# Keys by token for four units: made with TensorE transposes and a ScalarE copy instead of loaded

## The chip, the cores and the metric

One core of a Trainium2 chip runs the whole program; the other cores are idle. The metric is the device time of one execution in microseconds. Five engines work from queues of their own: TensorE (PE: weight loads and matmuls), VectorE (DVE), ScalarE (ACT), GpSimd (POOL) and SyncE (SP), which here issues all loads and stores. Engines wait for each other and for loads through semaphores.

## The reference, cut to what matters

Three stages follow one another; the change lies in the first.

```python
# 1. retention: batch 4, heads 8, sequence 576, head size 64
scores = (1 / sqrt(64)) * q @ k.transpose(0, 1, 3, 2)
gamma = 1 - 2.0 ** (-5 - arange(8))                  # one per head
Dmat = where(i >= j, gamma ** (i - j), 0)            # causal decay
x = (scores * Dmat) @ v                              # -> 2304 tokens x 512
# 2. h = x @ w_in (512 x 2048); g = h * sigmoid(1.702 * h); x = g @ w_out
# 3. h = x @ w_in2 (512 x 1024); solu = h * softmax(h); layer norm * g_ln; out = . @ w_out2
```

The outputs are 2304 x 512 numbers in fp32.

## The kernel before, in words

The retention is done in chunks. The 32 heads of the batch go two at a time: a *unit* is two heads (2 x 64 features on the 128 partitions), there are 16 units, and two units make a *pair* (`k` in `run`, 0 to 7). The sequence of 576 is four chunks of 128 tokens and a rest of 64. For a unit TensorE computes the following blocks:

- `scores` (line 394, tile `s`): inside each chunk, keys times queries, 4 chunks x 2 heads. VectorE masks them into SBUF (line 399).
- `states` (line 358, tile `T`): for each chunk, the sum over its tokens of key times value. This needs k *by token* (tokens on the partitions), while scores need k *by feature*. It also needs v scaled by the decay, which ScalarE does in place (`scale_v`, lines 343 and 347).
- `within` (line 409, tile `o`): masked scores times v.
- `across` (lines 424, 430 and 436, tiles `o` and `e`): the running state, which VectorE makes from `T` with a scan (line 367, once for a pair), times the queries. GpSimd has multiplied the queries by their decay before (`decay_q`, lines 328 and 333).
- `last_scores` (line 375, tile `e`): the scores of the rest of 64 tokens.

ScalarE or VectorE then copies the results from PSUM into `xb` (`take`, lines 447 to 454).

Each unit comes from memory in two loads that SyncE issues in order (`load_unit`, line 210). Part 0 is q and k by feature, 1152 columns. Part 1 is k by token (512 columns from `CKN`), and v (576 columns from `CV`): 1088 columns. So k is loaded twice, in two layouts. Six units have buffers (`NU`); unit 6 takes the buffers of unit 0 when these are free, and so on.

Nothing reorders the program: each engine's queue is filled in the order in which `run` calls the functions. Pair 0 has an order of its own (`EARLY = 1`): scores, T and `within` of unit 0 with short runs of idle matmuls between them (`spin`, tile `warm`), then scores and T of unit 1, the end scores, scores of unit 2, `within` of unit 1, `across` of the pair, then the T blocks of units 2 and 3, and scores of unit 3. Before the loop ScalarE scales the v of units 0 and 1; that of units 2 and 3 follows in pair 0. PSUM has four banks for `warm`, `T`, `o`, `e` (`bank`) and four for scores and others (`ybank`); a new tile in a bank waits until the one before is read.

The first part of stage 2 follows on directly: from the third pair on the first weights are loaded and converted beside the retention.

Of the kernel before, what the change touches and what calls it, by code (L numbers as in the profile page):

```python
# [13 lines left out]
ALU = mybir.AluOpType  # L14
# [3 lines left out]
B, H, S, D = 4, 8, 576, 64  # L18
# [5 lines left out]
P = 128  # L24
CH = 128
NCH = 4
# [15 lines left out]
CQ, CK = 0, S  # L42
CKN, CV = 2 * S, 2 * S + NCH * P
NV = 2 * NCH + 1
CATT = CV + NV * D
# [57 lines left out]
_M = {}  # L103
# [10 lines left out]

NU = 6
PLAIN = (0, 2)
EARLY = 1
NPAIR = B * NP // 2
IN_AT = [_M["att"], _M["att"] + CATT] + [_M["y"] + i * CATT for i in range(4)]
# [33 lines left out]
class Build:  # L153
# [56 lines left out]
    def load_unit(self, u, part):  # L210

        t = IN_AT[u % NU]
        a, b = ((0, CKN), (CKN, CATT))[part]
        self.load(t + a, self.att_in[u, :, a:b])

    def load_raw(self, dst, src):
# [118 lines left out]
    def scale_v(self, *units):  # L335
# [8 lines left out]
        for u in units:  # L344
            v = self.un(u)[0][:, CV:CATT]
            d = self.const("vdec")[:, u % NP * 3:u % NP * 3 + 3]
            self.nc.scalar.mul(v[:, n:], v[:, n:], d[:, 2:3])

    def states(self, u, pt):


        t = self.un(u)[0]
        n = NCH * D
        out = pt[:, u % 2 * n:(u % 2 + 1) * n].rearrange("r (e c) -> r c e", c=NCH)
        for c in range(NCH):
            for a, h in enumerate(self.rows(u)):
                w = slice(c * P + a * D, c * P + (a + 1) * D)
                self.nc.tensor.matmul(  # L358
                    out[h, c], t[:, CKN + w.start:CKN + w.stop], t[:, CV + w.start:CV + w.stop],
                    start=True, stop=True, skip_group_check=True,  # L360
                )

# [78 lines left out]
    def take(self, u, o, part):  # L441
# [3 lines left out]
        x = self.x(u)[:, n:S] if part else self.x(u)[:, 0:n]  # L445
        if u not in PLAIN:
            nc.scalar.copy(x, o[:, 0:LAST] if part else o)
# [249 lines left out]
    def run(self):  # L697
        nc = self.nc
# [7 lines left out]
        def spin(n):  # L706
            for _ in range(n):
                nc.tensor.matmul(wb[:, 0:P], warm, warm, start=True, stop=True)
# [9 lines left out]
        def load_w():  # L718
            f, h = raws.pop(0)
            n = slice(h * SLICE, (h + 1) * SLICE)  # L720
            self.load_raw(self.wraw[f][:, n], self.w1_in[f][:, h * DM:(h + 1) * DM])
# [2 lines left out]
        self.load_consts()  # L724
        self.load_unit(0, 1)
        self.load_decays(1, 1)
        self.fill_scan()
        for u in range(1, NU):
            for part in range(2):
# [6 lines left out]
        for f, h in halves:  # L736
            t = T_START[f % 2]
# [3 lines left out]
        for f in range(3, FH):  # L741
            t = T_START[f % 2]
# [4 lines left out]
            self.bg += [(0, p, "split") for p in self.split_weight(f, t)]  # L747


        self.scale_v(0)  # L750
        self.scale_v(1)
        self.decay_q(1)
        self.decay_q(3)
        for k in range(NPAIR):
            u = 2 * k
            nxt = k + 1 < NPAIR
            early = k < EARLY
            if k + 2 < NPAIR:
                self.decay_q(u + 4, u + 5)
            if nxt and not early:  # L760
                self.scale_v(u + 2, u + 3)
            if k != 1:
                self.scores(u)
            if k == 0:
                spin(4)
                pt = self.bank("T0")
                self.states(u, pt)
                spin(4)
                o = [self.bank("o0")]
                self.within(u, o[0], True)  # L770
                self.scores(u + 1)
                self.states(u + 1, pt)
                ends = self.bank("e0")
            else:
                self.scores(u + 1)
                if early:
                    pt = self.bank(f"T{k}")
                    for i in range(2):
                        self.states(u + i, pt)
                o = [self.bank(f"o{u}")]  # L780
                ends = self.bank(f"e{k}")
            if early:
                self.last_scores(k, ends)
                self.last_masks(k, ends)
                self.scan(k, pt)
                self.scores(u + 2)
            o.append(self.bank(f"o{u + 1}"))
            if early:
                for i in range(k == 0, 2):
                    self.within(u + i, o[i], True)  # L790
            if not nxt:
                self.split_x(0, 1, 0)
                self.split_x(0, 1, 1)
            self.background((0, 0, 0, 0, 2, 2, 2, 3)[k], True, nxt)
            ends = [ends, self.ybank(f"e{u + 1}")]
            self.across(k, o, ends, not early)
            if nxt and k >= EARLY - 1:
                self.last_scores(k + 1, ends[0])
                if early:
                    self.scale_v(u + 2, u + 3)  # L800
                pt = self.bank(f"T{k + 1}")
                self.states(u + 2, pt)
            for i in range(2):
                self.take(u + i, ends[i], True)
            if not nxt:
                self.emit_h(0, 0, 0, nc.vector, True)
                self.background(0)
            if not early:
                for i in range(2):
                    self.within(u + i, o[i], False)  # L810
            if nxt and k >= EARLY - 1:
                self.states(u + 3, pt)
                self.last_masks(k + 1, ends[0])
                self.background(k > 3)
                self.scan(k + 1, pt)
            for i in range(2):
                self.take(u + i, o[i], False)
                self.staged.add((4, u + i))
            if nxt and k < EARLY - 1:
                self.scale_v(u + 2, u + 3)  # L820
            for i in (u + NU, u + 1 + NU):
                if i < 2 * NPAIR:
                    for part in range(2):
                        self.load_unit(i, part)
            for _ in range((0, 0, 1, 1, 1, 1, 2, 2)[k]):
                load_w()
            if 2 < k < 7:
                self.split_x(0, 0, k - 3)
        prev, held = None, []
        for g, j, f in STEPS:  # L830
# [35 lines left out]
            if prev is not None:  # L866
                self.emit_y(*prev)
                pg, pj, pf = prev
                if pj == NB - 1:
# [3 lines left out]
                    elif pg == 2:  # L873
                        b = SLOT_OF[pf % FH]
# [179 lines left out]
```

## Time and profile before

| | us |
|---|---|
| median of 3 runs | 669.01 (668.78 to 669.54) |
| profiled execution | 669.22 |
| its span, first to last instruction | 667.4 |
| TensorE busy, share of the span | 658.9, 99% |
| VectorE busy | 487.1, 73% |
| GpSimd busy | 252.3, 38% |
| ScalarE busy | 232.7, 35% |

The profile is of one execution. Its page has busy times by engine, the span in 40 slices, the DMA queues, the chain of work that ended last, and groups of instructions. A busy TensorE is not TensorE at its peak, since matmuls overlap and their ends are modelled. One fp32 matmul of the program shows as two records (x16 is eight matmuls), a transpose as one. The retention ends at about 62 us of the span; the rest is stages 2 and 3.

### The profile page before, as it was taken

The numbers are of one execution on the slowest core, as the hardware profiler recorded it, in microseconds if no ns is written. First come the engines' busy times: TensorE is split into PE (matmuls) and PEld (weight loads), VectorE is DVE, ScalarE is ACT, GpSimd is POOL, SyncE is SP. The second block draws the span as 40 slices with busy tenths as digits, with TensorE's granted clock in tenths as the row PEclk, the third lists the DMA queues.
The fourth block names the chain that finished last, engine by engine and source line by source line (L and its number), as shares of the span: only waits on it lengthen the run. The fifth ranks groups of instructions, "written<-read, shape, count | busy, mean of one in ns | idle before, by whom it ended". The sixth has DMA issues, their size and how long they took to land.

```text
span 667.4 us, 10473 instructions
## 1 busy us (share of the span) xinstructions
PE 658.9 (99%) x4086; PEld 572.9 (86%) x4086; DVE 487.1 (73%) x769; ACT 232.7 (35%) x498; POOL 252.3 (38%) x268
## 2 busy tenths in 40 slices
PE   9999999999999999999999999999999999999998
PEld 8888888899888889998888888899878888888887
DVE  3678788688787866687675675467799987887780
ACT  2565544432112134121111211265545433543331
POOL 3465665534224149240220311289744322431200
PEclk9999999999999999999999999999999999999999
DMA  8998500012222210022211200000000000000001
GB/s 341 418 416 334 190 0 1 1 33 94 95 72 87 75 52 1 1 95 95 81 48 62 63 1 0 1 1 4 2 16 33 17 17 31 32 17 16 32 32 48
DMA packets 15025, 49.35 MB, mean 74 GB/s; under 512 B 1664, under 2 KB 2560, under 8 KB 14976
## 3 DMA queue, kind: packets, MB, share of 16 engines
q1 hardware_dynamic: 14976, 48.68, 20.0%
q8 instruction: 32, 0.52, 0.3%
q14 instruction: 17, 0.14, 0.1%
HBM read 43.96 MB, written 4.72 MB: 73 GB/s over the span
## 4 chain that ended last, share of the span: by engine, by line
PE 88%; DVE 5%; DMA 2%; issue 2%; ACT 1%; POOL 1%; SPq 0%; DVEq 0%; POOLq 0%; ACTq 0%
PE yp L523 28%; PE h L490 28%; PE o L688 14%; PE h L597 10%; DMA mem<-in_att 2%; PE zT L661 2%; PE s L394 2%; PE o L409 2%; PE T L358 1%; PE o L424 1%; DVE mem L603 1%; DVE mem L636 1%; DVE mem L562 1%; DVE mem L498 0%; ACT gs L500 0%
## 5 line engine op out<-in xcount | busy, mean ns | idle before, releaser
L490 PE MATMUL h<-xs,w 128*128 128x512 f32 (+1 forms) x960 | 212.1, 369 | 1.5 <-POOL xs L471 1.5
L523 PE MATMUL yp<-gs,w 128*128 128x512 f32 (+1 forms) x960 | 211.1, 368 | 0.3 <-ACT gs L500 0.3
L490 PEld LDWEIGHTS h<-xs,w 128*128 128x128 f32 x960 | 175.1, 188 | 26.6 <-POOL xs L471 4.0
L523 PEld LDWEIGHTS yp<-gs,w 128*128 128x128 f32 x960 | 175.0, 188 | 23.9 <-DVE mem L531 0.7
L471 POOL TENSOR_TENSOR xs<-xb,xs 128x384 fp32r<-128x384 f32 (+3 forms) x96 | 93.7, 1003 | 208.3 <-ACT xs L470 208.2
L497 ACT ACTIVATE mem<-h 128x512 f32<-128x512 f32 (+1 forms) x80 | 44.4, 555 | 257.3 <-PE h L490 257.2
L498 DVE TENSOR_TENSOR mem<-h,mem 128x512 f32<-128x512 f32 (+1 forms) x80 | 50.8, 636 | 86.2 <-ACT mem L497 86.0
L688 PE MATMUL o<-w,zs 128*128 128x512 f32 (+1 forms) x456 | 102.9, 382 | 0.0
L688 PEld LDWEIGHTS o<-w,zs 128*128 128x128 f32 x456 | 81.3, 188 | 15.1
L503 DVE TENSOR_TENSOR gs<-mem,gs 128x512 fp32r<-128x512 f32 (+1 forms) x80 | 68.2, 852 | 13.0 <-ACT gs L500 6.4
L259 POOL TENSOR_TENSOR w<-mem,w 128x512 fp32r<-128x512 f32 x34 | 45.9, 1377 | 25.2 <-ACT w L254 25.2
L559 POOL TENSOR_TENSOR ys_s<-mem,ys_s 128x256 fp32r<-128x256 f32 x36 | 35.0, 984 | 51.9 <-ACT ys_s L558 41.8
L502 DVE CAST gs<-mem 128x512 fp32r<-128x512 f32 (+1 forms) x69 | 41.6, 603 | 6.6
L597 PE MATMUL h<-wt,ys_s 128*128 128x512 f32 x162 | 41.3, 390 | 0.0
L603 DVE TENSOR_TENSOR mem<-h,mem 128x512 f32<-128x512 f32 x36 | 24.6, 687 | 21.1 <-PE h L597 12.5
L597 PEld LDWEIGHTS h<-wt,ys_s 128*128 128x128 f32 x162 | 30.3, 188 | 6.2
L648 POOL TENSOR_TENSOR mem<-mem 128x1 f32<-128x1 f32 x18 | 10.3, 572 | 64.7 <-DVE mem L647 64.7
L470 ACT CAST xs<-xb 128x384 fp32r<-128x384 f32 (+3 forms) x96 | 34.6, 432 | 0.0
L399 DVE SCALAR_TENSOR_TENSOR mem<-s,mem 128x512 f32<-128x512 f32 x32 | 21.9, 740 | 9.9 <-PE s L394 9.9
L671 DVE TENSOR_TENSOR zs<-zT,zs 128x512 fp32r<-128x512 f32 x36 | 23.1, 684 | 7.7 <-ACT zs L670 7.7
L597 PE MATMUL h<-wb,ys_a 128*128 128x512 f32 x108 | 27.6, 391 | 0.2 <-ACT mem L606 0.2
L640 DVE TENSOR_TENSOR mem<-mem 128x1024 f32<-128x1024 f32 x18 | 24.7, 1374 | 3.7 <-ACT mem L638 3.7
(82 smaller groups left out, 726.1 us busy)
## 6 DMA issues: line engine op xcount, KB each, us to landing
mem<-in_att SPq DMA_DIRECT2D x16, 576.0 KB, 7.6
mem<-in_att SPq DMA_DIRECT2D x16, 544.0 KB, 8.2
wraw<-in_w SPq DMA_DIRECT2D x16, 512.0 KB, 9.2
mem<-in_w SPq DMA_DIRECT2D x16, 512.0 KB, 3.7
out<-mem SPq DMA_DIRECT2D x17, 256.0 KB, 2.0
mem<-in_w2in SPq DMA_DIRECT2D x8, 512.0 KB, 3.7
mem<-in_w2out SPq DMA_DIRECT2D x8, 512.0 KB, 3.7
out<-mem SPq DMA_DIRECT2D x2, 128.0 KB, 1.7
```

The costliest lines, as they stand in the source:

```text
L259: nc.gpsimd.tensor_tensor(lo[:, c], w[:, c], f32(hi[:, c]), ALU.subtract)
L470: nc.scalar.copy(t[:, 0, done:done + n], x)
L471: nc.gpsimd.tensor_tensor(t[:, 1, done:done + n], x, f32(t[:, 0, done:done + n]), ALU.subtract)
L490: nc.tensor.matmul(h[:, 0:width], a[:, w], x[:, b, 0:width], start=(n == 0), stop=(n == 3 * KB - 1))
L497: nc.scalar.activation(g, h[:, 0:width], AF.Sigmoid, scale=1.702)
L498: nc.vector.tensor_tensor(g, h[:, 0:width], g, ALU.mult)
L502: nc.vector.tensor_copy(gs[:, 0], g)
L503: lo_engine.tensor_tensor(gs[:, 1], g, f32(gs[:, 0]), ALU.subtract)
L523: nc.tensor.matmul(o, a[:, w], gs[:, b], start=(first and i == 0), stop=(last and i == 2))
L559: nc.gpsimd.tensor_tensor(ys[:, 1], src, f32(ys[:, 0]), ALU.subtract)
L597: nc.tensor.matmul(o, a[:, l, k], m[:, w], start=(start and i == 0), stop=(stop and i == 5), skip_group_check=True,)
L688: nc.tensor.matmul(o[:, 0:n], z[:, a, k], b[:, c:c + n], start=(k == 0 and i == 0), stop=(k == FB - 1 and i == 2),)
```

## The change: k by token from k by feature, for units 0 to 3

For units 0 to 3 (`TURNED`) part 1 of the load begins at `CV` and leaves k by token out. In its place `turn_k` transposes the four chunks of k by feature on TensorE, into one PSUM bank (tile `kn`), and ScalarE copies the bank, 128 x 512, to where the load used to put it. For a transpose an identity matrix is needed; GpSimd makes it from the constant `tri` (a triangle of ones) by subtracting the triangle shifted by one column. In units with an odd number the two heads stand the other way round on the partitions, so `states` picks its columns by `h` there. The scalings of v move behind these copies in ScalarE's queue. Units 4 to 15 are loaded as before.

```diff
+TURNED = 4
@@ load_unit
-        a, b = ((0, CKN), (CKN, CATT))[part]
+        a, b = ((0, CKN), (CKN if u >= TURNED else CV, CATT))[part]
@@
+    def turn_k(self, u):
+        nc = self.nc
+        t = self.un(u)[0]
+        ident = self.at(_M["g"] + 2 * P, P)
+        pt = self.bank(f"kn{u}")
+        for c in range(NCH):
+            w = slice(c * P, (c + 1) * P)
+            nc.tensor.transpose(pt[:, w], t[:, CK + c * CH:CK + (c + 1) * CH], ident)
+        nc.scalar.copy(t[:, CKN:CV], pt)
@@ states
+                k = CKN + (c * P + h.start if u < TURNED else w.start)
-                    out[h, c], t[:, CKN + w.start:CKN + w.stop], t[:, CV + w.start:CV + w.stop],
+                    out[h, c], t[:, k:k + D], t[:, CV + w.start:CV + w.stop],
@@ run
+        ident, tri = self.at(_M["g"] + 2 * P, P), self.const("tri")
+        nc.gpsimd.tensor_copy(ident[:, 0:1], tri[:, 0:1])
+        nc.gpsimd.tensor_tensor(ident[:, 1:], tri[:, 1:], tri[:, 0:P - 1], ALU.subtract)
         self.fill_scan()
...
-        self.scale_v(0)
-        self.scale_v(1)
         self.decay_q(1)
...
+            if k == 0:
+                self.turn_k(0)
+                self.scale_v(0)
             if k != 1:
                 self.scores(u)
...
                 self.within(u, o[0], True)
+                self.turn_k(1)
+                self.scale_v(1)
                 self.scores(u + 1)
...
                 self.scan(k, pt)
+                self.turn_k(2)
                 self.scores(u + 2)
...
                 if early:
-                    self.scale_v(u + 2, u + 3)
+                    self.scale_v(u + 2)
+                    self.turn_k(3)
+                    self.scale_v(u + 3)
                 pt = self.bank(f"T{k + 1}")
                 self.states(u + 2, pt)
```

ScalarE's queue before, from the scalings of unit 0 to the first results of pair 0. Line 343 scales the four chunks of one head, line 347 the rest of 64 tokens; the names in brackets are the semaphores that a row waits for, and DMAHW ones are loads.

```order
L343 ACTIVATE mem<-mem 128x4x64 [waits DMAHW2_49,DMAHW1_49]
L343 ACTIVATE mem<-mem 128x4x64
L347 ACTIVATE mem<-mem 128x64
L343 ACTIVATE mem<-mem 128x4x64 [waits DMAHW5_49]
L343 ACTIVATE mem<-mem 128x4x64
L347 ACTIVATE mem<-mem 128x64
L343 ACTIVATE mem<-mem 128x4x64 [waits DMAHW0_49]
L343 ACTIVATE mem<-mem 128x4x64
L343 ACTIVATE mem<-mem 128x4x64 [waits DMAHW3_49]
L343 ACTIVATE mem<-mem 128x4x64
L347 ACTIVATE mem<-mem 128x64 x2
L447 COPY xb<-e_225 128x64 [waits PE_49]
```

The same place after the change, units 1 to 3. Line 359 is the copy of the transposed k, and the lines that were 343, 347 and 447 are 344, 348 and 460.

```order
L359 COPY mem<-kn_181 128x512 [waits PE_49]
L344 ACTIVATE mem<-mem 128x4x64 [waits DMAHW5_49]
L344 ACTIVATE mem<-mem 128x4x64
L348 ACTIVATE mem<-mem 128x64
L359 COPY mem<-kn_218 128x512 [waits PE_49]
L344 ACTIVATE mem<-mem 128x4x64 [waits DMAHW0_49]
L344 ACTIVATE mem<-mem 128x4x64
L348 ACTIVATE mem<-mem 128x64
L359 COPY mem<-kn_273 128x512 [waits PE_49]
L344 ACTIVATE mem<-mem 128x4x64 [waits DMAHW3_49]
L344 ACTIVATE mem<-mem 128x4x64
L348 ACTIVATE mem<-mem 128x64
```

Each unit's scalings, which waited for a load alone, now stand behind a copy that waits for TensorE.

TensorE's queue before, at the end of pair 0: the end scores of units 2 and 3 (line 375), the T blocks of units 2 and 3 (line 358), and the scores of unit 3 (line 394).

```order
L375 MATMUL e_196<-mem 64x64 [waits DMAHW2_49,Pool_49]
L375 MATMUL e_196<-mem 64x64
L358 MATMUL T_256<-mem 64x64 [waits DMAHW0_49,PE_49,Activation_49]
L358 MATMUL T_256<-mem 64x64 [waits Activation_49]
L358 MATMUL T_256<-mem 64x64 x6
L358 MATMUL T_256<-mem 64x64 [waits DMAHW3_49,Activation_49]
L358 MATMUL T_256<-mem 64x64 [waits Activation_49]
L358 MATMUL T_256<-mem 64x64 x6
L394 MATMUL s_0_294<-mem 128x128 [waits Pool_49]
```

The same place after: line 358 is now the transpose, line 371 the T blocks, line 388 the end scores, line 407 the scores.

```order
L388 MATMUL e_210<-mem 64x64 [waits DMAHW2_49,Pool_49]
L388 MATMUL e_210<-mem 64x64
L358 MATMUL kn_273<-mem 128x128 x4
L371 MATMUL T_282<-mem 64x64 [waits DVE_49,DMAHW0_49,PE_49,Activation_49]
L371 MATMUL T_282<-mem 64x64 [waits Activation_49]
L371 MATMUL T_282<-mem 64x64 x6
L371 MATMUL T_282<-mem 64x64 [waits DMAHW3_49,Activation_49]
L371 MATMUL T_282<-mem 64x64 [waits Activation_49]
L371 MATMUL T_282<-mem 64x64 x6
L407 MATMUL s_0_320<-mem 128x128 [waits Pool_49]
```

The four transposes of unit 3 stand directly ahead of the T blocks of units 2 and 3, and the T block of unit 3 waits for what ScalarE does behind them.

## Rows read from the trace of the kernel before

**Rows 1.** The page: busy us of each engine, share, instructions.

```profile
PE 658.9 (99%) x4086; PEld 572.9 (86%) x4086; DVE 487.1 (73%) x769; ACT 232.7 (35%) x498; POOL 252.3 (38%) x268
```

**Rows 2.** By stretch: busy us (instructions) of each engine, granted clock, DMA share, GB/s.

```profile
5.40:20.00 14.60, 13.66 (x234) 11.79 (x233) 7.34 (x14) 5.56 (x15) 3.69 (x8) 1.00 1.01 401
20.00:62.00 42.00, 40.42 (x898) 38.04 (x901) 32.68 (x55) 24.57 (x69) 24.85 (x32) 1.00 1.02 417
62.00:667.40 605.40, 600.48 (x2946) 518.77 (x2942) 446.94 (x701) 201.08 (x413) 222.07 (x223) 1.00 0.12 41
```

**Rows 3.** The chain of waits, 0 to 60 us: start, us, what.

```profile
8.47 9.80 DMA mem<-in_att
...
18.34 0.31 POOL mem L328
...
18.65 1.23 DVE mem L367
...
20.02 1.00 PE o L424 x24
...
24.53 1.99 PE s L394 x32
```

**Rows 4.** TensorE in order of time: start, us, engine, line, what [idle before].

```profile
5.45 1.16 PE L394 MATMUL s<-mem 64*128 64x128 f32 x16
6.54 1.16 PE L708 MATMUL warm<-mem 128*128 128x128 f32 x8
7.63 0.95 PE L358 MATMUL T<-mem 128*64 128x64 f32 x16
8.51 1.16 PE L708 MATMUL warm<-mem 128*128 128x128 f32 x8
11.71 0.68 PE L358 MATMUL T<-mem 128*64 128x64 f32 x16
12.33 0.45 PE L375 MATMUL e<-mem 64*64 64x64 f32 x8
16.27 0.69 PE L358 MATMUL T<-mem 128*64 128x64 f32 x16
17.47 1.08 PE L358 MATMUL T<-mem 128*64 128x64 f32 x16 [0.51 <-ACT mem L343]
18.48 1.16 PE L394 MATMUL s<-mem 64*128 64x128 f32 x16
```

**Rows 5.** ScalarE in order of time: scalings of unit 3, a copy from PSUM.

```profile
16.91 0.91 ACT L343 ACTIVATE mem<-mem 128x256 f32<-128x256 f32 x2 [3.27 <-DMA mem<-in_att]
18.29 0.58 ACT L447 COPY xb<-o 128x512 f32<-128x512 f32 x1
```

**Rows 6.** GpSimd and VectorE in order of time.

```profile
0.73 0.95 POOL L200 MEMSET mem<- 128x1024 f32 x1 [0.29 <-POOLq L1044]
4.89 1.21 POOL L204 COPY mem<-mem 128x192 f32<-128x192 f32 x4 [3.21 <-DMA mem<-in_consts]
8.59 0.30 POOL L328 TENSOR_TENSOR mem<-mem 128x64 f32<-128x64 f32 x1 [2.49 <-DMA mem<-in_att]
8.85 1.09 POOL L333 TENSOR_TENSOR mem<-mem 128x512 f32<-128x512 f32 x1
18.65 1.22 DVE L367 TENSOR_TENSOR_SCAN mem<-mem,T 128x512 f32<-128x512 f32 x1 [1.77 <-POOL mem L328]
```

**Rows 7.** The page: the instruction queue (packets, MB, share); DMA issues (KB, median us to landing).

```profile
q8 instruction: 32, 0.52, 0.3%
...
mem<-in_att SPq DMA_DIRECT2D x16, 576.0 KB, 7.6
mem<-in_att SPq DMA_DIRECT2D x16, 544.0 KB, 8.2
```

**Rows 8.** TensorE and ScalarE at 481 us: eight transposes, the next block, the copy.

```profile
481.16 1.03 PE L661 MATMUL zT<-mem 128*128 128x128 f32 x8
481.95 0.48 PE L597 MATMUL h<-wt,ys_a 128*128 128x512 f32 x1
...
481.79 0.59 ACT L670 CAST zs<-zT 128x512 fp32r<-128x512 f32 x1 [2.74 <-PE zT L661]
```

**Rows 9.** TensorE in order of time: `across` of pairs 2, 3 and 7.

```profile
26.45 1.00 PE L424 MATMUL o<-mem 64*64 64x128 f32 x24
32.77 1.00 PE L424 MATMUL o<-mem 64*64 64x128 f32 x24
60.98 1.00 PE L424 MATMUL o<-mem 64*64 64x128 f32 x24
```

**Rows 10.** The chain of waits, 30 to 60 us: what it calls issue.

```profile
34.68 0.36 issue
...
40.91 0.24 issue
...
53.23 0.39 issue
...
59.15 0.52 issue
```

**Rows 11.** Waits of TensorE from 62 us on: us in total, times, longest.

```profile
PE h L490 <- POOL xs L471: 1.5, 2, 0.8
PE yp L523 <- ACT gs L500: 0.3, 1, 0.3
PE h L597 <- ACT mem L606: 0.2, 1, 0.2
```

## The prediction

> **What bounds the kernel now.** I read the page's busy table first: TensorE is busy 658.9 of 667.4 us [rows 1], so nearly everything that is added to TensorE's own queue, or put in front of it, is paid in full, and a load matters only where TensorE waits for it. The table by stretch says where that could be: loads run at 401 GB/s from 5.4 to 20 us, at 417 GB/s until 62 us, and at 41 GB/s in the 605 us after that [rows 2]. The change touches the first 20 us alone. The chain of waits follows a load there up to 18.27 us, then a scan on VectorE, and TensorE from 20.02 us on [rows 3], which would make loads the bound of the start. The rows of TensorE in order of time say less. Its blocks follow one another from 5.45 us to the T block at 16.27, and it loses time at three places [rows 4]. The T block of unit 0 lasts from 7.63 to 8.51 us, 0.88, where an undisturbed one goes from 11.71 to 12.33, 0.62: 0.26 us lost. The T block of unit 3 would begin at 16.27 + 0.62 = 16.89 and end at 17.51; it ends at 18.48, 0.97 us late, because ScalarE's two scalings of v begin only at 16.91, when their load has landed [rows 5]. And `across` at 20.02 waits for the scan that ends at 18.65 + 1.22 = 19.87 [rows 6]; 18.48 + 1.09 (a block of scores, 5.45 to 6.54) would be 19.57, so 0.45 us. The chain names a GpSimd operation at 18.34 as what released this scan; the T block itself ends at 17.47 + 1.08 = 18.55, just ahead of 18.65, and is the likelier releaser.
>
> So loads cost TensorE about 1.7 us here, not the 10 us that the chain puts to them.
>
> **What is removed.** Part 1 of units 0 to 3 loses 512 of its 1088 columns: of 544 KB [rows 7], 288 KB stay. 256 KB are 0.262 MB, at 417 GB/s 0.63 us for each unit; the v of unit 3, and every load behind it while the queue stays full, lands 4 x 0.63 = 2.5 us sooner. Of this TensorE can take back at most those 1.7 us.
>
> **What is added on TensorE.** 16 transposes of 128x128. The kernel has such transposes late in the program: eight go from 481.16 to the start of the next block at 481.95, so 0.10 us each [rows 8]. Four take 0.4. A change of the block's shape costs too: one block of scores takes 1.09, a double one 1.99 [rows 3, 4], so one change is 2 x 1.09 - 1.99 = 0.2. Unit 0's four stand where the shape changes anyway; for units 1 to 3 I add 0.2 each. In all 4 x 0.4 + 3 x 0.2 = 2.2 us, all of it in TensorE's queue.
>
> The Trainium skill gives a transpose inside a kernel about 275 ns ("TensorE: Matmul & The Clock Gate", Part 4: PE-mode transpose). The row here agrees with that as the length of one, and shows that eight in a row overlap; taken one behind the other, 16 would be 4.4 us instead of 1.6 before changes of shape.
>
> **What is added in front.** *The identity.* GpSimd makes it once the constants have landed, 4.89 today [rows 6]: a copy of one column and a subtraction of 127. There is no such row; a multiplication takes 0.30 with 64 columns and 1.09 with 512 [rows 6], so about 0.4, and with a column's copy 0.5 (between 0.3 and 1.1 for both). Transposes then start near 5.6 instead of 5.45: 0.2 us, between 0 and 0.7. The table that GpSimd fills afterwards has its rows' 0.95 and 1.2 still ahead of 8.59, when it is next wanted.
>
> *The copy and the scalings.* ScalarE's order becomes copy, scale, scale for each unit (its rows are shown with the change). A 128x512 copy from PSUM takes 0.58, the two scalings 0.91 [rows 5]. T needs all three. Before, a unit's scalings ran as soon as its v had landed, under TensorE's other work; now they stand behind a copy that waits for TensorE. From the start of the last transpose to the end of the second scaling: 0.27 (one transpose) + 0.08 (hand-over: the copy at 481.79 behind a group that ends near 481.7 [rows 8]) + 0.58 + 0.91 = 1.84 us.
>
> **The sum, as lateness of TensorE against today.** Unit 0: 0.2 for the identity, 0.4 for transposes, and the 0.26 of T's wait gone: +0.35. Unit 1: transposes 0.6, so +0.95; the last one starts at about 11.4, the scalings end at 13.2, where T could begin at 11.71 + 0.95 = 12.66; +0.5, so +1.45. Unit 2: transposes 0.6; its copy hides under scores and `within`; +2.05. Unit 3: its transposes, 0.6 more, stand directly ahead of the T block of unit 2, which begins at 16.27 + 2.65 = 18.9. The last one starts at about 18.65, the scalings end at 18.65 + 1.84 = 20.5. T of unit 2 covers 0.6 of that, the rest is bare: T of unit 3 goes from 20.5 to 21.1, where it ends at 18.48 today: **+2.6 us**. The wait for the load is gone, and a longer one for ScalarE has come in its place. Scan and `across` follow, at 22.6 instead of 20.02. Bounds: with no cost for a change of shape and a free identity the same steps give +2.1; with the identity at 0.7, +3.1.
>
> **Behind 20 us.** Is this paid to the end? From 26.45 to 32.77 a pair of units takes 6.32 us with TensorE full; from 32.77 to 60.98 four pairs take 28.21, which is 2.93 more than 4 x 6.32 [rows 9]. That excess might give something back. The chain puts it to no engine: gaps called issue, 0.36, 0.24, 0.39 and 0.52 us, inside blocks [rows 10]. TensorE's list of waits after 62 us, where loads are few, has none [rows 11], and there is a queue that loads instructions, 32 packets, 0.52 MB [rows 7]. I take the gaps as TensorE waiting for its instructions behind a deep queue of data; that is an inference. This queue becomes shallower: loads are 2.5 us sooner, and TensorE frees the buffers for later units 2.6 us later, together 5.1 of the 7.6 us from issue to landing [rows 7]. So the excess shrinks by something between nothing and 2.9. No row shows a half-full queue, and the queue stays busy through most of the stretch; I take 1.1, a good third. +2.6 - 1.1 = +1.5. After 62 us nothing absorbs it: TensorE is full but for 2.0 us of waits [rows 11], which hang on the same work.
>
> The profiled execution took 669.22 us, 667.4 of it span and 1.8 around it, 0.2 above the median of 669.01. 669.0 + 1.5 = 670.5.
>
> **Rivals.**
> *The gaps close (no change).* If instructions arrive in time once the queue is shallow, all 2.9 come back: 669.0 + 2.6 - 2.9 = 668.7, or 669.7 with two thirds. For it: no such gap with an idle queue. Against: from 20 to 32 us TensorE ran the same blocks with loads at the same rate and lost nothing, so a busy queue alone isn't enough for a gap, nor then perhaps its absence.
> *Loads are the bound (faster).* If the chain is right and copies and scalings hide, TensorE gets back 1.7 us of waits against 2.2 + 0.2 of transposes and identity, +0.7, and with 2.5 of the 2.9 from the gaps it is -1.8: 667.2. It decides from the second pair's `across` at 20.9 or sooner. Against it: T of unit 3 has only one T block, 0.6 us, to hide 1.84 behind.
> *Transposes in series (slower by more).* If each of the 16 waits out the 0.27 us of the one before, they add 16 x 0.17 = 2.7, and the gaps give back 1.1: 669.0 + 2.6 + 2.7 - 1.1 = 673.2. It decides from 0.2 us between starts on. Against it: the eight at 481 us.
>
> **How the numbers follow.** The forecast, +0.7 to +2.6 (669.7 to 671.6), has 0.50; gaps that close 0.27; loads as the bound 0.11; series 0.07; gaps that grow, above 671.6, 0.05. A measurement of this kernel tells about 0.2%, 1.3 us, from no change, so 670.35 is the line. Of the forecast's half 0.37 lies above it; with the last two, slower has 0.49. Same takes 0.13 and 0.25 of the closing gaps, 0.38; faster 0.02 and 0.11, 0.13. The range, 668.7 to 672.2, leaves out loads as the bound and the series, 0.18, and little else.
>
> **What would show it.** Right: each four transposes within 0.45 us; ScalarE's copy of unit 3 and two scalings that end near 20.5, TensorE idle about 1 us ahead of the T block of unit 3 and named as waiting for ScalarE, `across` near 22.6; from there to the block that is at 60.98 today, some 1.1 us less than today's 40.96. Wrong: that `across` at or before 20.9, so that the copy is hidden; or the same 40.96 us behind it (nothing given back), or 38.0 (all).

## The result, and the profile after

| | before | after |
|---|---|---|
| median, runs side by side | 669.16 us (668.78 to 670.35) | 672.42 us (672.11 to 674.0) |
| ratio | | 1.0054 (95%: 1.0044 to 1.0064) |
| profiled execution, span | 669.22, 667.4 | 672.41, 670.6 |

The kernel became slower by 0.54%, 3.3 us on the medians and 3.2 us on the spans. The forecast was 670.5, its range 668.7 to 672.2: the direction came as foretold, the size lies above the range.

The page after, beside [rows 1]: busy us, share, instructions.

```profile
PE 660.4 (98%) x4102; PEld 573.7 (86%) x4102; DVE 486.9 (73%) x769; ACT 234.9 (35%) x502; POOL 252.7 (38%) x270
```

TensorE's busy time grew by 1.5 us and the span by 3.2, so half of the loss is time in which TensorE stands still. The table by stretch after, with the columns of [rows 2], says where.

```profile
5.40:20.00 14.60, 14.04 (x216) 11.77 (x216) 6.20 (x12) 5.85 (x15) 6.84 (x14) 1.00 0.93 353
20.00:62.00 42.00, 38.82 (x860) 36.48 (x860) 30.75 (x52) 24.29 (x69) 20.01 (x27) 1.00 0.99 380
62.00:670.60 608.60, 603.60 (x3006) 521.73 (x3006) 449.81 (x704) 203.24 (x419) 225.17 (x226) 1.00 0.13 43
```

Loads went down to 353 and 380 GB/s, from 401 and 417. But between 20 and 62 us TensorE is busy for 38.82 us, where it was for 40.42: with fewer loads it stands still for longer.

TensorE after, in order of time, beside [rows 4]: start, us, line, tile, [idle before].

```profile
5.57 0.66 PE L358 MATMUL kn<-mem 128*128 128x128 f32 x4 [0.57 <-POOL mem L742]
6.15 1.16 PE L407 MATMUL s<-mem 64*128 64x128 f32 x16
8.33 0.69 PE L371 MATMUL T<-mem 128*64 128x64 f32 x16
8.95 1.16 PE L721 MATMUL warm<-mem 128*128 128x128 f32 x8
...
18.33 0.66 PE L358 MATMUL kn<-mem 128*128 128x128 f32 x4
19.20 0.69 PE L371 MATMUL T<-mem 128*64 128x64 f32 x16 [0.21 <-PE kn L358]
20.07 1.07 PE L371 MATMUL T<-mem 128*64 128x64 f32 x16 [0.18 <-ACT mem L344]
21.07 1.16 PE L407 MATMUL s<-mem 64*128 64x128 f32 x16
22.52 1.00 PE L437 MATMUL o<-mem 64*64 64x128 f32 x24 [0.29 <-DVE mem L380]
...
57.36 1.00 PE L437 MATMUL o<-mem 64*64 64x128 f32 x24
64.31 1.00 PE L437 MATMUL o<-mem 64*64 64x128 f32 x24
```

The start went nearly as worked out: `across` of the second pair begins at 22.52 (20.02 before), 2.50 later. From there to the last `across` it is 64.31 - 22.52 = 41.79 us, where it was 60.98 - 20.02 = 40.96 [rows 4, 9]. So 2.50 + 0.83 = 3.33 us, which is the whole loss.

GpSimd and ScalarE after, beside [rows 5, 6]: the identity, then unit 3's copy and scalings.

```profile
4.89 0.19 POOL L741 COPY mem<-mem 128x1 f32<-128x1 f32 x1 [4.45 <-DMA mem<-in_consts]
5.12 0.39 POOL L742 TENSOR_TENSOR mem<-mem 128x127 f32<-128x127 f32 x1
...
19.02 0.59 ACT L359 COPY mem<-kn 128x512 f32<-128x512 f32 x1 [2.53 <-PE kn L358]
19.51 0.91 ACT L344 ACTIVATE mem<-mem 128x256 f32<-128x256 f32 x2
```

The second scaling ends at 20.42; the copy follows the transposes that began at 18.33, and T of unit 3 follows the scaling.

What the chain of waits after calls issue, beside [rows 10].

```profile
42.33 0.84 issue
...
49.12 0.46 issue
...
55.01 1.04 issue
...
61.59 0.47 issue
```

Four gaps of 2.81 us together, where the four before had 1.51. The gaps did not shrink; they grew and stand elsewhere. They grew by 1.30 and the distance by 0.83: a wait can also hide in a longer block, as at 46.48 before, where `across` takes 1.42 us for 21 of its 24 rows (1.00 for all elsewhere).

### The profile page after: what moved, and what is told of

Same layout as the page of the kernel before. It is cut to its first block, busy times and chain, and to the rows that moved or that the text cites. A ratio compares the mean times of both kernels' runs of the same rounds, so it can differ in the third digit from the quotient of the medians.

```text
span 670.6 us, 10512 instructions
## 1 busy us (share of the span) xinstructions
PE 660.4 (98%) x4102; PEld 573.7 (86%) x4102; DVE 486.9 (73%) x769; ACT 234.9 (35%) x502; POOL 252.7 (38%) x270
## 4 chain that ended last, share of the span: by engine, by line
PE 89%; DVE 5%; issue 2%; ACT 2%; POOL 1%; DMA 1%; SPq 0%; DVEq 0%; POOLq 0%; ACTq 0%
PE yp L536 28%; PE h L503 27%; PE o L701 14%; PE h L610 10%; PE zT L674 2%; PE s L407 2%; PE o L422 2%; PE T L371 1%; PE o L437 1%; DVE mem L616 1%; DMA mem<-in_consts 1%; DVE mem L649 1%; DVE mem L575 1%; DVE mem L511 0%; ACT gs L513 0%
## 5 line engine op out<-in xcount | busy, mean ns | idle before, releaser
L510 ACT ACTIVATE mem<-h 128x512 f32<-128x512 f32 (+1 forms) x80 | 44.5, 556 | 257.1 <-PE h L503 252.7
L572 POOL TENSOR_TENSOR ys_s<-mem,ys_s 128x256 fp32r<-128x256 f32 x36 | 35.0, 984 | 51.9 <-ACT ys_s L571 41.8
```

The lines of the kernel that those rows point to most:

```text
L510: nc.scalar.activation(g, h[:, 0:width], AF.Sigmoid, scale=1.702)
L572: nc.gpsimd.tensor_tensor(ys[:, 1], src, f32(ys[:, 0]), ALU.subtract)
```

## The experiments

Where a distance is given, it is from `across` of the second pair to the last `across`, as above.

### The start: which piece costs what

**e1: the added work alone.** Transposes and copies as in the change, but k by token is loaded too.

```diff
-        a, b = ((0, CKN), (CKN if u >= TURNED else CV, CATT))[part]
+        a, b = ((0, CKN), (CKN, CATT))[part]
```

> The changed kernel with the loads of units 0 to 3 whole again: identity, transposes, copies and the moved scalings stay, the copy writes over the k by token that was loaded. Theory S (the start is TensorE's queue and ScalarE's copies behind it, loads matter nowhere any more): across of the second pair at 22.5 us as in the changed kernel, within 0.2, although the v of unit 3 lands some 2.5 us later (16.9). Rival L (shorter loads already give back part of the cost): 1 to 2.5 us later, 23.5 to 25. Behind it, theory Q (the gaps on TensorE have grown because the loads are now paced by TensorE and come in bursts): from there to the across of the last pair about 40.9 as in the kernel before, so time near 671.6. Rival P (the gaps have grown because 32 more TensorE instructions move the places where its instruction blocks end): 41.8 as in the changed kernel, time 672.4.

Measured: ratio 1.0052 (1.0035 to 1.0068), `across` of the second pair at 22.51, distance 41.42, between the 40.9 and the 41.8 that were expected. The 1 MB of loads that the change saves is worth nothing for the start: it is as late with the saving as without.

**e2: the removed loads alone.** The kernel before without the loads of k by token for units 0 to 3; VectorE fills their place with a constant.

```diff
-        a, b = ((0, CKN), (CKN, CATT))[part]
+        a, b = ((0, CKN), (CKN if u >= 4 else CV, CATT))[part]
+        for u in range(4):
+            nc.vector.memset(self.un(u)[0][:, CKN:CV], 0.01)
```

> The kernel before with the shorter loads of units 0 to 3 and nothing else: their k by token is left out and holds a constant that VectorE writes at the start, so the states of these units are wrong. Theory S: TensorE's three waits of the start go (0.26 + 0.97 + 0.45), across of the second pair at 18.3 to 18.9 instead of 20.02; no more, although loads are 2.5 us sooner. Rival L (loads bound the start as the chain of waits says): 17.5. Behind it, theory Q: the queue of loads is shallower by 2.5 us only, TensorE earlier: distance to the last across about 40.9 to 41.8, time 667.5 to 668.7. Rival P: no TensorE instruction is added, so 40.9 exactly as before, 667.7.

Measured: ratio 0.9985 (0.9972 to 0.9997). TensorE's rows in e2:

```profile
5.62 1.69 PE L394 MATMUL s<-mem 64*128 64x128 f32 x16
...
16.70 1.15 PE L358 MATMUL T<-mem 128*64 128x64 f32 x32
...
19.34 1.00 PE L424 MATMUL o<-mem 64*64 64x128 f32 x24 [0.40 <-DVE mem L367]
```

The T blocks of units 2 and 3 run on in one, without the wait of [rows 4], and `across` is 0.68 sooner, not the 1.1 to 1.7 that S had; part of the gain went into a slow first block (1.69 instead of 1.16). The distance is 40.63 where before it was 40.96, with no TensorE instruction added or taken away, and at the last `across` (59.97) the lead is 1.01 us. At 79.39, where the block `yp` that began at 79.68 before stands, it is 0.29. The rows of VectorE in between show why: its conversion of weights at line 237 ends at 64.99 instead of 65.26, and the products at line 498 that TensorE waits for stand behind it. So all that the loads could ever give back was about 1 us, and most of that is lost to VectorE after 62 us.

**e3: unit 3's transposes ahead.** In the changed kernel they move from the end of pair 0 to behind the scores of unit 2, the scalings of unit 2 ahead of them.

```diff
+                self.scale_v(u + 2)
                 self.scores(u + 2)
+                self.turn_k(3)
+                self.scale_v(u + 3)
```

> The changed kernel with the transposes of unit 3 moved up, from directly ahead of the T blocks of units 2 and 3 to behind the scores of unit 2, and the scalings of unit 2 ahead of them on ScalarE. Theory S: copy and scalings of unit 3 hide under within and across of the first pair; T of unit 3 no longer waits, across of the second pair at 21.4 to 21.6 instead of 22.5. Rival T (what costs is TensorE's own work alone, 2.2 us): 22.4. Time, if the gaps stay as in the changed kernel: 671.4.

Measured: 671.23 us, ratio 1.0033 (1.0017 to 1.005), 1.2 below the change. `across` of the second pair is at 21.89, T of units 2 and 3 in one block with no wait. 0.63 of the 0.92 us that the wait for ScalarE costs (worked out below) came. The rest was lost elsewhere: the wait for the scan took 0.40 instead of 0.29, and the very first transposes, which this run did not move, took 0.93 instead of 0.58. Behind that this profile can't be compared: the granted clock was 0.88 from 50 to 60 us and 0.91 from 60 to 65.

**e4: e3, and no idle matmuls.** Also without the two `spin(4)`, and the transposes of unit 1 ahead of `within` of unit 0.

```diff
-                spin(4)
                 pt = self.bank("T0")
                 self.states(u, pt)
-                spin(4)
+                self.turn_k(1)
+                self.scale_v(1)
                 o = [self.bank("o0")]
                 self.within(u, o[0], True)
-                self.turn_k(1)
-                self.scale_v(1)
```

> As the run before, and the two fillers of four idle matmuls each between scores, T and within of unit 0 are taken out, with the transposes of unit 1 ahead of within of unit 0 where the second filler stood. Theory S: the fillers are TensorE time (2 x 1.09) that now stands on the path, since the loads have run ahead: across of the second pair at 19.3 to 19.6, ahead of the 20.02 of the kernel before; time 668.3 to 669.5 by the gaps. Rival C (the fillers keep the clock up; without them TensorE falls to half its rate at a wait): blocks of scores of 2 us instead of 1.1, across of the second pair after 22. Rival L (loads still bound): no earlier than 20.0.

Measured: 669.05 us, ratio 0.9994 (0.9984 to 1.0003): no longer slower than before.

```profile
17.05 1.15 PE L371 MATMUL T<-mem 128*64 128x64 f32 x32
...
19.69 1.00 PE L437 MATMUL o<-mem 64*64 64x128 f32 x24 [0.40 <-DVE mem L380]
...
61.54 1.00 PE L437 MATMUL o<-mem 64*64 64x128 f32 x24
```

`across` is 0.33 sooner than before the change and 2.8 sooner than with it. Of these 2.8 us e3 had 0.63 by order; the other 2.20 came with the idle matmuls gone, which last 2 x 1.09, and with the transposes of unit 1 moved, and no run tells these two apart. The distance, 41.85, is close to the changed kernel's.

**e8: the kernel before, no idle matmuls.** To see whether e4's gain is only that.

```diff
-                spin(4)
                 pt = self.bank("T0")
                 self.states(u, pt)
-                spin(4)
```

> The kernel before without its two fillers of four idle matmuls in pair 0. Theory S: TensorE reaches the T block of unit 3 by 2.2 us sooner and waits there for the load, which lands at 16.9 as ever: across of the second pair at 19.9 to 20.0, time within 0.5 us of before. So the 2.2 us of fillers are free there, and not free in the changed kernel, where run four took them out. Rival F (fillers cost what they last): across at 17.9, 667.

```profile
17.73 1.08 PE L358 MATMUL T<-mem 128*64 128x64 f32 x16 [1.29 <-ACT mem L343]
```

Measured: 669.81 us, ratio 1.0017 (1.0001 to 1.0033), `across` of the second pair at 20.28. The wait of T of unit 3 grows from 0.51 to 1.29, since its load lands when it does: in the kernel before the idle matmuls fill a wait and cost nothing. In the changed one, which waits for no load there, e4 gets time back by leaving them out.

### Behind 20 us: what the gaps are

The page says that 32 packets of instructions were loaded, 0.52 MB [rows 7], so 16 KB each. TensorE's 4086 matmuls and 4086 weight loads [rows 1] are 8172 instructions, 255 for each packet, if all packets are TensorE's. An fp32 matmul is four of these (two rows of PE, two of PEld), a transpose two: the change adds 32 ahead of the gaps. Theory P: the gaps are waits for such packets behind the data loads, and their length hangs on where in the blocks of work a packet ends. Rivals: the number of instructions ahead (Q), or the later start and the other order (O). (In the expectations up to e9, Q stands for the pace and the depth of the loads, or for what moved with them; from e10 on it is the number of instructions.)

**e6 and e7: few loads.** The kernels before and after, the loads of units 6 to 15 cut to 64 columns for each part.

```diff
+        if u >= NU:
+            b = a + 64
```

> The kernel before with the loads of units 6 to 15 cut to 64 columns for each part; the rest of their data is left out (they compute on what their buffers held), and everything else is as it was. If the gaps are TensorE waiting for instructions behind loads (both P and Q hold that), they go: 37.6 to 37.9 us from across of the second pair to across of the last instead of 40.96, span 664 to 664.5. If they are TensorE's own (rival O), 40.9 stays.

> The changed kernel with the same cut of the loads of units 6 to 15 (their data is left out). Gaps from instructions behind loads: 37.6 to 37.9 us between those two places instead of 41.8, and a span of about 666.6, so that what is left against the kernel before with the same cut is the start alone, +2.5. Rival O: 41.8 stays.

TensorE and the table by stretch in e6, then in e7:

```profile
20.30 1.00 PE L426 MATMUL o<-mem 64*64 64x128 f32 x24 [0.38 <-DVE mem L369]
...
58.54 1.00 PE L426 MATMUL o<-mem 64*64 64x128 f32 x24
```

```profile
20.00:62.00 42.00, 41.55 (x916) 39.55 (x916) 35.51 (x59) 24.95 (x71) 25.79 (x34) 1.00 0.54 172
```

```profile
22.89 1.00 PE L439 MATMUL o<-mem 64*64 64x128 f32 x24 [0.29 <-DVE mem L382]
...
60.94 1.00 PE L439 MATMUL o<-mem 64*64 64x128 f32 x24
```

At 172 GB/s instead of 417 TensorE is busy for 41.55 of 42 us, and the distances are 38.24 and 38.05; the list of TensorE's waits has no issue in either. So the excess, 2.7 us before and 3.7 after, comes from the loads, in both kernels alike; O, as a cost of its own, is out. In this stretch of e6 TensorE has 1832 rows in 42 us, a packet of 255 every 5.8 us. The DMA queues of the kernel before from 20 to 62 us (packets, MB, share) show seven such packets among the data:

```profile
q1 hardware_dynamic: 4502, 17.38, 101.4%
q8 instruction: 7, 0.11, 1.0%
```

No row names a packet as what ended a gap, but counting the rows and looking up the packets does. Here is what each engine had done from the start of the program to where each gap begins, columns as in [rows 2], first in the kernel before and then in the changed one:

```profile
0.00:34.68 34.68, 32.67 (x596) 29.91 (x596) 18.30 (x33) 15.00 (x40) 13.05 (x25) 1.00 0.96 380
0.00:40.91 40.91, 38.54 (x722) 35.46 (x722) 21.88 (x40) 19.26 (x51) 16.43 (x30) 1.00 0.97 387
0.00:53.23 53.23, 50.58 (x971) 46.72 (x971) 32.67 (x58) 26.25 (x70) 24.14 (x40) 1.00 0.98 393
0.00:59.15 59.15, 56.10 (x1096) 51.90 (x1097) 37.87 (x66) 29.87 (x80) 27.46 (x43) 1.00 0.99 395
...
0.00:42.33 42.33, 39.89 (x721) 36.08 (x721) 21.52 (x39) 20.96 (x55) 16.32 (x32) 1.00 0.91 335
0.00:49.12 49.12, 45.83 (x845) 41.69 (x846) 26.71 (x48) 25.28 (x66) 19.68 (x36) 1.00 0.93 346
0.00:55.01 55.01, 51.26 (x971) 46.79 (x971) 32.07 (x56) 27.61 (x73) 23.14 (x41) 1.00 0.94 353
0.00:61.59 61.59, 56.80 (x1096) 52.01 (x1096) 37.12 (x65) 31.22 (x83) 27.11 (x45) 1.00 0.95 359
```

The gaps of both kernels stand behind the same numbers of TensorE's rows, PE and PEld together, about 250 apart, although the work at these places differs by 32 rows. Before: 1192, 1444, 1942, 2193. After: 1442, 1691, 1942, 2192. With the semaphore instructions in its queue, which the views leave out, the places lie 256 apart. And the instruction packets in the DMA records of the two traces (queue q8, us):

| | packet begins | packet ends | TensorE goes on | later by |
|---|---|---|---|---|
| before | 32.61 | 33.49 | 35.04 | 1.55 |
| | 38.68 | 39.62 | 41.15 | 1.53 |
| | 51.36 | 52.28 | 53.62 | 1.34 |
| | 57.27 | 58.23 | 59.67 | 1.44 |
| after | 40.93 | 41.87 | 43.18 | 1.31 |
| | 47.24 | 48.17 | 49.58 | 1.41 |
| | 53.75 | 54.68 | 56.05 | 1.37 |
| | 59.88 | 60.85 | 62.06 | 1.21 |

The profiles of both kernels and of the fifteen experiments have 60 such gaps (over 0.12 us) between 20 and 64 us. All stand at these places, each ends 1.2 to 1.6 us behind the end of a packet, and that packet had begun 3.4 to 5.5 us after TensorE passed the place before. With few loads (e6, e7) packets begin 0 to 3.1 us after it, and there is no gap. So the gaps are waits for packets behind loads. The first half of P is shown. As to its second half, the places stay where they are; how long a gap is follows above all from how late its packet begins: 0.13 to 0.68 us where it began up to 3.8 us after the place before, 0.84 to 1.86 where it began 4.7 us after it or later.

The times were 667.81 and 669.95, spans 666.0 and 668.2: 2.2 us apart, the start's 2.59 of `across` and little else.

The Trainium skill says that a sequencer fetches its instructions in blocks of 256 (16 KiB) while it executes the block before, and that crossing a block's end is mostly hidden ("Runtime: NRT & Kernel Launch", Instruction fetch mechanics). The trace agrees on the size. It does not agree on the hiding while loads run at 417 GB/s: 40.96 us against 38.24.

**e5, e10, e14, e13, e15, e9: the same work, more or fewer instructions ahead.** e5 puts 8 idle matmuls of one column into TensorE's wait ahead of T of unit 3, e10 8 more ahead of `across`; e14 and e13 put 42 and 74 of them at the very start in place of the ten there; e15 and e9 make one matmul of 512 columns of each `spin(4)`, in the kernel before and in the changed one.

```diff
+                if k == 0:                       # e5
+                    for _ in range(8):
+                        nc.tensor.matmul(
+                            ends[0][0:32, 448:449], warm[:, 0:32], warm[:, 0:1], start=True, stop=True, skip_group_check=True
+                        )
...
-                spin(4)                          # e15, e9
+                nc.tensor.matmul(wb, warm, self.un(0)[0][:, 0:512], start=True, stop=True)
```

> The kernel before with eight tiny matmuls (32 columns of weights, one column moved, into an unused part of a bank) ahead of the T block of unit 3, where TensorE waits for a load for 0.5 us and more: 32 more TensorE records, as many as the 16 transposes bring, at the same place in the program, and nothing else. Across of the second pair stays at 20.0 to 20.3. Rival P (the places where TensorE's instruction blocks end set the gaps): gaps after that as in the changed kernel and the run with the work alone, first one of 0.8 to 1.0 us near 40 us, and 41.4 to 41.8 us from across of the second pair to across of the last. Theory Q (the pace and depth of the loads sets them): 40.9, first gap near 34 us, as before.

> The changed kernel with each of its two runs of four idle fp32 matmuls (16 records) replaced by one idle matmul of 512 columns (about the same time on TensorE, 4 records). TensorE's queue then has 8 records more than the kernel before where across of the second pair stands, instead of 32. Theory P (the gaps' length hangs on where in the blocks of work an instruction load ends, so on the count of records): across of the second pair near 22.5 as in the changed kernel, the distance to the last across near the 40.96 of before, time 671.3 to 671.8. Theory Q (the distance of 41.8 comes from the lateness of the start or from the loads that moved, not from the count): distance 41.5 to 42.0, time 672.2 to 672.6.

> The kernel before with 16 tiny idle matmuls (64 records): 8 ahead of the T block of unit 3, 8 ahead of across of the second pair; together about 0.5 us of TensorE, of which the first 8 lie in a wait. With 8 of them (32 records) the distance from across of the second pair to the last across was 42.20 instead of 40.96. Theory P (position decides, up and down): the distance is another one again, by at least 0.4 us from both, after up to 0.3 us of the second 8 is taken off; a direction is not foretold. Theory Q (more records, more instructions to load, so longer in proportion): 43.0 to 43.6, time 671.5 to 672.2.

> The kernel before with the ten idle fp32 matmuls at the very start (40 records) replaced by 74 idle ones of one column (296 records): 256 records more ahead of everything, which is what one packet of instructions holds if 32 packets serve the whole program. They take about 0.07 us each, 5.2 us instead of 4.4, more at a low clock: the start may be 1 to 4 us late, so the distance from across of the second pair to the last across is what is compared. Theory P (position in the blocks decides): a whole block more changes nothing: 40.5 to 41.5 (40.96 before). Theory Q (it grows with the count ahead): 32 records gave 1.24 and 64 gave 2.1, so 256 give 7 to 9: 48 to 50.

> The same with 42 idle matmuls of one column in place of the ten: 128 records more, about 3 us instead of 4.4, so no lateness at the start. Distance from across of the second pair to the last across. Theory P: not above what 64 gave by more than 0.5, so 40.5 to 43.5. Theory Q: 3.5 to 5 more than the 40.96 of before: 44.5 to 46.

> The kernel before with each run of four idle fp32 matmuls replaced by one of 512 columns: 24 records fewer, the same time on TensorE. Theory P: the distance is another one than 40.96; with 24 records fewer the changed kernel lost 1.1 of its distance, without the fillers altogether (32 fewer) it was 40.52: 40.0 to 40.8, time 668.3 to 669.0. If neither position nor count matters this early: 40.96 and 669.2.

Instructions are counted against the kernel before; distances are from one profile each.

| kernel | instructions | `across` of second pair | last `across` | distance | median us | ratio (95%) |
|---|---|---|---|---|---|---|
| e8 | -32 | 20.28 | 60.80 | 40.52 | 669.81 | 1.0017 (1.0001 to 1.0033) |
| e15 | -24 | 19.61 | 63.62 | 44.01 | 672.05 | 1.0037 (1.0021 to 1.0054) |
| before | 0 | 20.02 | 60.98 | 40.96 | 669.27 | 1 |
| e5 | +32 | 20.04 | 62.24 | 42.20 | 670.50 | 1.002 (1.001 to 1.003) |
| e10 | +64 | 20.61 | 63.67 | 43.06 | 671.13 | 1.0027 (1.0014 to 1.004) |
| e14 | +128 | 20.65 | 64.89 | 44.24 | 673.18 | 1.0056 (1.0041 to 1.007) |
| e13 | +256 | 23.74 | 64.58 | 40.84 | 674.97 | 1.0082 (1.0069 to 1.0095) |
| e9, changed | +8 | 22.65 | 63.35 | 40.70 | 672.10 | 1.0042 (1.0028 to 1.0055) |
| after | +32 | 22.52 | 64.31 | 41.79 | 672.42 | 1.0054 (1.0044 to 1.0064) |

TensorE in e13:

```profile
23.74 1.00 PE L424 MATMUL o<-mem 64*64 64x128 f32 x24 [0.40 <-DVE mem L367]
...
64.58 1.00 PE L424 MATMUL o<-mem 64*64 64x128 f32 x24
```

The times of e9 and e10 were compared with 669.27 for the kernel before, those of e5 and e8 with 669.33, those of e13 to e15 with 669.05, and the changed kernel's with 669.16.

e5 starts no later and still lost 1.2 us: 32 instructions that lie in a wait are enough. Its distance is above P's 41.4 to 41.8, and its first gap is at 28.46, not near 40. Up to 128 the distance grows, as Q has it (44.24 in e14, between P's limit of 43.5 and Q's 44.5); with 256, a whole packet more, it is back at 40.84, where Q had 48 to 50. Q is out. But position is not all: e15, 24 fewer, had 40.0 to 40.8 by P and has 44.01, with gaps from 24.29 on where before the first stands at 34.68. And its runs fall into two groups, four from 669.1 to 669.6 and eight from 671.8 to 674.3: one and the same program takes one course or another. The packet that ends its gap at 24.29 begins 5.4 us after TensorE passed the place before (23.23, 17.79); in the kernel before the same packet begins 3.4 us after it (20.86, 17.47). So the excess over a stretch with few loads (38.24) is 2.3 to 6.0 us among the kernels of the table, and one profile of each is a thin basis: e9 is 1.1 shorter than the changed kernel by its profile but only 0.3 by its median, which the intervals don't tell apart. Which course a kernel takes I could not foretell.

### A better version

**e11 and e12: e4 with fewer units.** As e4, with transposes for units 0 and 1, and for unit 0 alone.

```diff
-TURNED = 4
+TURNED = 2                                       # e12: 1
```

> The reordered version with transposes for units 0 and 1 alone (units 2 and 3 load k whole), both runs of idle matmuls left out, unit 1's transposes ahead of within of unit 0. Transposes of units 2 and 3 cost 2 x 0.6 us in TensorE's queue and a copy ahead of the scalings of unit 3. Theory S (each piece of the start adds up as in the traces): across of the second pair at 18.4 to 18.9, about 1.4 us ahead of the kernel before. Theory L (loads bound the start once idle matmuls are gone): 19.7 or later, as with four units. Behind that, with a distance of 41.0 to 42.0 and a part of the lead lost to VectorE after 62 us: time 667.7 to 669.0 by S, 669.0 to 669.6 by L.

> As the reordered version, with transposes for unit 0 alone. Theory S: unit 1's transposes (0.6 us) leave TensorE's queue, but its T block then waits for its whole load as in the kernel before; across of the second pair at 18.2 to 18.9, time 667.5 to 669.0. Theory L: 19.7 or later, time 669.0 to 669.6.

Measured: e11 669.5 us, ratio 1.0002 (0.9989 to 1.0015), `across` of the second pair at 19.14, distance 41.56; e12 671.37, 1.0026 (1.001 to 1.0041), 19.62. S was 0.24 short in e11 and L is out there: 0.88 sooner than before. The gaps take 0.6 of it back; the profiled execution keeps the rest (668.87), the median of twelve runs does not. In e12 T of unit 3 waits 0.66 for ScalarE, whose load comes later again; its distance is 44.91, part of it at a lower granted clock (last section). But for e6, a single run with most loads left out, none of the fifteen beats the kernel before by more than the 0.15% of e2, and that one can't be had, since k by token is needed.

## Why the prediction was right or wrong

**The start: right, term by term.** The identity took 0.58 on GpSimd (0.5 foretold) and put the first block 0.12 later (0.2); most of the 0.57 that TensorE stands idle for it comes from its idle matmuls, which end half a us sooner here than in the kernel before. The transposes with their change of shape take 0.58 for each unit (5.57 to 6.15 above; foretold were 0.6 for units 1 to 3 and 0.4 for unit 0). T of unit 0 no longer loses anything (8.33 to 8.95, 0.62). From the last transposes at 18.33 the chain of copy and scalings ends at 20.42, foretold 20.5; without waits T of unit 3 would end at 18.33 + 0.58 + 0.62 + 0.62 = 20.15, and it ends at 21.07: 0.92 us lost, about 1 foretold. Only 0.18 of it stands as a wait for ScalarE. Another 0.38 is inside the block, which takes 1.07 instead of 0.69, so the group's mark alone would hide it, and 0.29 lies ahead of T of unit 2, where the profile names the transposes; but the second scaling, which T of unit 3 needs, ends at 20.42 in any case. e3 shows the cause: with the transposes moved ahead neither block waits. `across` came at 22.52 (22.6).

**The rivals of the start.** Transposes in series: refuted, 0.58 for four with the change of shape. (With the 275 ns of the Trainium skill, "TensorE: Matmul & The Clock Gate", Part 4: PE-mode transpose, taken one behind the other, four would by that estimate be 1.1 us; the trace agrees with it only as a length, 0.27 us for one, and their starts are 0.11 apart.) Loads as the bound: e1 and e2 refute it; without the added work the removed loads bring `across` to 19.34, and with it nothing. The gaps close: refuted, 2.81 us of them are there.

**Behind 20 us: wrong.** The step that failed is "the excess shrinks by something between nothing and 2.9 ... I take 1.1". It grew by 0.83, so the term was off by 1.9 us, which is the whole miss (672.4 against 670.5). The inference on which it stood, that the gaps are TensorE waiting for instructions behind data, is borne out: without the data they are gone (e6, e7), and each ends behind the end of a packet. What failed is the way from there to a size. I let the gaps follow the depth of the queue of data, and this queue is emptier only ahead of the gaps. The changed kernel by stretch, columns as in [rows 2]:

```profile
30.00:40.00 10.00, 10.00 (x234) 9.61 (x228) 6.26 (x13) 5.48 (x16) 2.75 (x5) 1.00 0.91 331
40.00:50.00 10.00, 8.70 (x184) 8.05 (x184) 8.40 (x15) 6.78 (x19) 6.57 (x9) 1.00 1.01 397
50.00:62.00 12.00, 10.55 (x246) 9.89 (x242) 9.52 (x17) 5.84 (x17) 6.96 (x9) 1.00 1.02 414
```

At 331 GB/s TensorE is busy throughout; the gaps stand where the loads are back at 397 and 414. The packets show the same: those at 26.87 and 31.89 begin 1.7 and 1.3 us after TensorE passed the place before (3.0 and 3.6 in the kernel before), and the four behind 40 us 3.8 to 4.8 us after it (3.6 to 3.9 before). I also took the instructions as given, and the change itself put 32 more into TensorE's stream. The kernel before shows that this alone can cost 1.2 us (e5), and the changed one with 24 fewer has its 0.83 back in its profile (40.70, e9), though not in its median. Growth of the gaps had 0.05 in the chances, though the start with unchanged gaps already gives 671.6; a change of their sum should have had like chances on both sides of that.

**What stays open.** What makes a packet wait 3.4 us behind full loads in one place and 5.4 in another, and so why 24 instructions fewer give 44.01 us and 32 fewer 40.52, and why one program has two courses. Only profiles of many executions of one kernel could show that, and there is one for each.

## What to carry to other kernels

Follow a change of the start block by block: durations of the same operations elsewhere in the program gave the lateness of TensorE to 0.1 us over 17 us. Where full loads meet a dense stream of small matmuls, the waits for instructions added up to 3 us more with a few dozen instructions fewer ahead of them (e15), and to 2 us more with a few dozen more (e10): give a change ahead of such a stretch that spread, on both sides. To tell such a gap from others, count the engine's rows up to it and look for the instruction packet that ended just ahead of where the engine goes on. A copy on an idle engine is free by its share and still costs its length where another engine needs it next; one block sooner, and with the idle matmuls gone, it cost nothing (e4).

## What the runs showed that was not expected

- After one-column matmuls at the start (e14, 84 rows in 4.6 us) the first block of scores takes 2.08 us and the next idle block 2.07, against 1.16 each before, though the granted clock of 5.6 to 10 us reads 1.00. In e2 the first block took 1.69.
- The granted clock of some profiled runs falls for a stretch around 60 us. The table by stretch in e12:

```profile
50.00:60.00 10.00, 9.91 (x228) 9.36 (x224) 8.12 (x13) 5.29 (x17) 5.24 (x7) 1.00 1.02 416
60.00:70.00 10.00, 8.40 (x110) 7.55 (x106) 9.90 (x14) 4.05 (x11) 7.07 (x8) 0.83 0.74 283
```

TensorE is busy for 9.91 of the first 10 us and for 8.40 of the second, and 0.83 is a mean of the two levels, 1.2 and 2.4 GHz. That run took 675.39 us; the fastest of the same kernel took 669.37. In e13 it is 0.91 from 80 to 100 us, behind waits of 1.39 and 0.72 us.
- Leads won before 60 us don't last: e2's 1.01 us were 0.29 at 79 us, and of the 2.44 by which e6 leads at the last `across` its span keeps 1.4.
